# Attention and the first unit's group 0: from separate loops to one list of operations with needs, ranks and durations

## The chip, the cores and the metric

The kernel runs on one core of a Trainium2 chip. The core has a matrix engine (TensorE, PE in the profile, with its weight loads shown apart as PEld), a vector engine (VectorE, DVE), a scalar engine (ScalarE, ACT), a general engine (GpSimd, POOL) and a sync engine (SyncE, SP) that here only issues DMA transfers. Each engine works through its own queue in order and waits at an instruction until the semaphores it needs have come. The metric is the device time of one execution in microseconds: 676.35 us before, the median of 3 runs from 675.85 to 676.41.

## The reference, cut to what matters

Three stages follow one another: windowed attention with a slope per head, a layer of four weighted experts, and a gated layer behind a norm.

```python
# attention: batch 2, heads 8, seq 576, head_dim 64, window 128
scores = scale * np.matmul(q, k.transpose(0, 1, 3, 2))
scores = np.where(mask, scores + bias[None], -1000000000.0)
scores = scores - np.max(scores, axis=-1, keepdims=True)
attn = np.exp(scores)
attn = attn / (np.sum(attn, axis=-1, keepdims=True) + 1e-09)
attn_out = np.matmul(attn, v)
x = attn_out.transpose(0, 2, 1, 3).reshape(1152, 512)
# experts: x (1152, 512), w1 (4, 512, 1024), w2 (4, 1024, 512)
p = domain_probs / (domain_probs.sum(-1, keepdims=True) + 1e-09)
for e in range(4):
    h = np.maximum(x @ w1[e], 0.0)
    out += p[:, e:e + 1] * (h @ w2[e])
# gated layer: rms norm, silu(xn @ w_gate) * (xn @ w_val) @ w_out
```

## The kernel before, in words

**Attention** (lines 297 to 413) goes over 8 pairs of heads, called pair 0 to 7 here: 2 batches times 4 pairs. For each pair, `load_pair` fetches keys and queries (`kt`, `qt`) and, for every second pair, values (`vt`). `scores` takes the 576 rows in 9 row blocks of 64: PE multiplies into the PSUM tile `s` (L337), DVE adds the bias and finds the least value (L346), ACT takes the exponential (L350), DVE makes the reciprocals for 5 and then 4 row blocks (L359, L360), and POOL scales (L362). The rows lie in one of two buffers, `tt` and a part of `y`, in turn. `values` transposes them on PE into `pst` (L383), ACT or DVE copies them out into `pt` and `pe` (L369, L371; which engine is written down as `"dadad"`), and PE multiplies them with the values into `po` (L389) and the end of `pst` (L406). The result is split into two parts, `xh` by ACT (L412) and `xl` by DVE (L413). So PE uses three shapes of its array here: 64*64 for `s`, 128*64 for `po` and the products of L406, and 128*128 for transposes and all that follows.

**Fillers.** Tokens come in two groups of 576, one for each batch. The first half of expert 0 (the first unit) is computed plainly: `hidden` (L226) makes `h` from `x` and `w1`, 12 matmuls of 288 columns into `psa` for each of 8 blocks of group 0, and `mixed` (L419) makes 4 output tiles of 12 matmuls into `psb`, after it has split `h` into two parts, ACT first (L179) and then POOL (L180). The weights are split the same way. Then `sums` (L431) makes 7 operands for the later units out of sums of quarters of `x`: 12 operations of 128x576 on DVE and 4 on ACT, on `scratch`.

**What sets the order.** In this part the code only says in which order things are recorded: pair by pair, scores one pair ahead of values, one of the `sums` behind every second row block, two fillers behind each pair of the second batch, the rest at the end. A scheduler of the language then orders each engine's instructions. Behind the attention a planner (`Plan`, L49) decides, and from the mark at L521 on each of PE, DVE, ACT and POOL is held to the recorded order by added dependencies (L1160 to L1169). The first work behind the attention is group 1 of the first unit: 8 blocks of 12 matmuls into `ps_a` to `ps_d` (by the helper's line, L209), then 5 output tiles (L901), then the units of products (L783).

Of the kernel before, what the change touches and what calls it, by code (L numbers as in the profile page):

```python
# [24 lines left out]
P = 128  # L25
# [120 lines left out]

@with_exitstack
def tile_fused(ctx: ExitStack, tc: tile.TileContext, qS, kS, vS, probs, w1, w2, wgv, wo, g, out):
# [87 lines left out]
    def load_probs():  # L236
        nc.sync.dma_start(out=pr_sb, in_=probs)
        nc.vector.tensor_reduce(out=psm, in_=pr_sb, op=ALU.add, axis=mybir.AxisListType.X)
# [23 lines left out]
    with (  # L262
# [34 lines left out]
        def load_pair(b, p):  # L297
            qt = qk_p.tile([P, S], F32, tag="q", name="qt")
            kt = qk_p.tile([P, S], F32, tag="k", name="kt")
            nc.sync.dma_start(out=kt, in_=kS[b, p])  # L300
            state["dma"] = nc.sync.dma_start(out=qt, in_=qS[b, p])
            if p % 2 == 0:
# [4 lines left out]
                state["vt"] = vt  # L307
            if b == 0:
                for r in range(2):
                    rows = slice(r * D, (r + 1) * D)  # L310
                    for i, eng in enumerate((nc.vector, nc.gpsimd)):
                        eng.tensor_scalar(
                            out=bias[rows, p, i, :], in0=rel[rows], scalar1=-8.0 * 2.0 ** (-8.0 * (2 * p + (r ^ i) + 1) / H),
                            scalar2=1.0, op0=ALU.mult, op1=ALU.mult,
                        )
            return qt, kt, state["vt"]

        def scores(n, p, qt, kt):
            tt = tts[n % 2]
            st = st_p.tile([P, 4, NQ], F32, tag="st", name="st")  # L320
            spans = []
            sps = []

            def pair(t0):

                ts = range(t0, min(t0 + 2, NQ))
                for t in ts:
                    k0 = max(0, t - 2) * D
                    nk = (t + 1) * D - k0
                    sps.append(ps_s.tile([P, 4 * D], F32, tag="s", name="s")[:, :nk])  # L330
                    c0 = WIN - nk + (D if t % 2 else 0)
                    spans.append(tt[:, t, c0 : c0 + nk])
                for t in ts:
                    k0 = max(0, t - 2) * D
                    for r in range(2):
                        rows, o = slice(r * D, (r + 1) * D), (r ^ t & 1) * D
                        nc.tensor.matmul(  # L337
                            sps[t][o : o + D, :], lhsT=qt[rows, t * D : (t + 1) * D], rhs=kt[rows, k0 : (t + 1) * D],
# [3 lines left out]
            for t in range(NQ):  # L342
                if t % 2 == 0:
                    pair(t)
                nk = sps[t].shape[1]
                nc.vector.tensor_tensor_reduce(  # L346
                    out=spans[t], in0=sps[t], in1=bias[:, p, t % 2, WIN - nk :], scale=-0.125, scalar=3.0e38,
                    op0=ALU.add, op1=ALU.min, accum_out=st[:, 0, t : t + 1],
                )
                nc.scalar.activation(  # L350
                    out=spans[t], in_=spans[t], func=AF.Exp, bias=st[:, 0, t : t + 1], scale=-1.0,
                    accum_out=st[:, 1, t : t + 1],
                )
                if t % 2:
                    some(1)
                if t + 1 in (5, 9):
                    g0 = (5, 9)[(5, 9).index(t + 1) - 1] if (5, 9).index(t + 1) else 0
                    gs = slice(g0, t + 1)
                    nc.vector.tensor_scalar(out=st[:, 2, gs], in0=st[:, 1, gs], scalar1=1e-9, scalar2=None, op0=ALU.add)  # L359
                    nc.vector.reciprocal(out=st[:, 3, gs], in_=st[:, 2, gs])  # L360
                    for j in range(g0, t + 1):
                        nc.gpsimd.tensor_scalar(  # L362
                            out=spans[j], in0=spans[j], scalar1=st[:, 3, j : j + 1], scalar2=1.0, op0=ALU.mult, op1=ALU.mult,
                        )
            return tt

        def evac(eng, out, in_):
            if eng == "a":
                nc.scalar.activation(out=out, in_=in_, func=AF.Copy)  # L369
            else:  # L370
                nc.vector.tensor_copy(out, in_)  # L371

        def values(b, p, tt, vt):
            pt = pt_p.tile([P, 4, 4, P], F32, tag="pt", name="pt")
            pe = pt_p.tile([D, P], F32, tag="pe", name="pe")
            po = ps_o.tile([P, 4 * P], F32, tag="po", name="po")
            for kb in range(5):
                n = min(4, NQ - 2 * kb)
                nk = D if kb == 4 else P
                pst = ps_t.tile([P, 4, P], F32, tag="pst", name="pst")  # L380
                for j in range(n):
                    c0 = P if j < 2 else 0
                    nc.tensor.transpose(pst[:nk, j, :], tt[:, 2 * kb + j, c0 : c0 + nk], ident)  # L383
                dst = pe if kb == 4 else pt[:, kb, :n, :]
                evac("dadad"[kb], dst, pst[:nk, 0, :] if kb == 4 else pst[:, :n, :])

                def mm(j, out, rhs, start, stop):
                    v = slice((2 * p % 4 + j) * D, (2 * p % 4 + j + 1) * D)
                    nc.tensor.matmul(  # L389
                        out, lhsT=vt[:nk, kb, v], rhs=rhs, start=start, stop=stop, skip_group_check=True,  # L390
                    )

                if kb < 4:
                    m = 4 if kb < 3 else 2
                    blocks = pt[:, kb, :m, :].rearrange("p (a b) (c d) -> p a (b c) d", b=2, c=2)
                    for j in range(2):
                        r = slice(j * D, (j + 1) * D)
                        mm(j, po[r, kb * P : kb * P + m * D], blocks[:, :, 1:3, :] if j else blocks[:, :, ::3, :], kb == 0, kb == 3)
                else:
                    pp = pst[:, 2, :D]  # L400
                    for kk in (3, 4):
                        for j in range(2):
                            r = slice(j * D, (j + 1) * D)
                            v = slice((2 * p % 4 + j) * D, (2 * p % 4 + j + 1) * D)
                            n = P if kk == 3 else D
                            nc.tensor.matmul(  # L406
                                pp[r, :], lhsT=vt[:n, kk, v], rhs=pt[:, 3, 2, r] if kk == 3 else pe[:, r],
                                start=kk == 3, stop=kk == 4, skip_group_check=True,
                            )
            for ps, w, o in ((po, 4 * P, 0), (pp, D, 4 * P)):  # L410
                c = slice(b * S + o, b * S + o + w)
                nc.scalar.activation(out=xh[:, p, c], in_=ps, func=AF.Copy)  # L412
                nc.vector.tensor_tensor(out=xl[:, p, c], in0=ps, in1=xh[:, p, c].bitcast(F32), op=ALU.subtract)  # L413

        def filler():
            w = blocks["w1_0"]
            v = blocks["w2_0"]

            def mixed(t):  # L419
                a = token_parts(op_p.tile([P, 2, 512], F32R, tag="oa", name="op"), t, "ap")  # L420
                ps = ps_a0.tile([P, DM], F32, tag="a", name="psb")
                gemm_out(ps, a, v)
                nc.vector.tensor_scalar(out=y[:, t, :], in0=ps, scalar1=pn_sb[:, t, :1], scalar2=None, op0=ALU.mult)

            for c in range(4):
                for t0 in (0, 288):
                    yield lambda c=c, t0=t0: hidden(ps_a0, w, c, t0, 288)
            for t in range(4):
                yield lambda t=t: mixed(t)

        def sums():  # L431

            st = [scratch()[:, :S].rearrange("p (a b) -> p a b", a=2) for _ in range(2)]
            (ah, al), (bh, bl), (ch, cl), (dh, dl) = ([x.bitcast(F32) for x in second(n, 0)] for n in (0, 1, 2, 4))

            def tt(op, out, a, b):
                return lambda: nc.vector.tensor_tensor(out=out, in0=a, in1=b, op=op)

            def keep(n, i):
                hi, lo = second(n, 0)  # L440
                yield lambda: nc.scalar.activation(out=hi, in_=st[i], func=AF.Copy)
                yield tt(ALU.subtract, lo, st[i], hi.bitcast(F32))

            yield tt(ALU.subtract, st[0], ch, dh)
            yield tt(ALU.add, st[0], st[0], cl)
            yield tt(ALU.subtract, st[0], st[0], dl)
            yield from keep(6, 0)
            yield tt(ALU.subtract, st[0], dh, ah)
            yield tt(ALU.add, st[0], st[0], dl)
            yield tt(ALU.subtract, st[0], st[0], al)  # L450
# [751 lines left out]
```

## Time and profile before

| what | before |
|---|---|
| time, median of 3 runs | 676.35 us (675.85 to 676.41) |
| the profiled execution's own time | 676.36 us |
| its span, first to last instruction | 674.6 us |
| granted TensorE clock | 1.000 |
| PE busy | 663.5 us (98% of the span) |
| DVE, ACT, POOL busy | 512.8, 312.2, 54.6 us |
| first matmul of group 1 starts (`ps_b`, L209) | 95.81 us |

The first 95.81 us of the span are the part that the change touches; from there on the chain that ended last runs on PE nearly without a break. Busy time of PE is read with care: a matmul counts from its start to its modelled end, matmuls overlap, and a matmul that stands in the array while the next shape waits counts as busy too. So in this part the starts of successive rows say more than the busy share.

### The profile page before, as it was taken

The page shows a single profiled execution, that of the slowest core. Times are in us where ns is not written, and L with a number is a line of the kernel's source. Part 1 is how long each engine was busy: PE and PEld are TensorE (multiplying, and loading weights), DVE is VectorE, ACT ScalarE, POOL GpSimd, SP SyncE. Part 2 cuts the span into 40 slices and gives each one's busy share as a digit, 9 for nine tenths or more (in the row PEclk, how much of TensorE's full clock was granted, in tenths as well). Part 3 has the DMA queues.
Part 4 walks back from the last instruction along what each step waited for, and adds up shares of the span by engine and source line. Part 5 has one row for each costly group of instructions (what it writes and reads, how often), then busy time and mean ns, then how long its engine had stood idle before and what let it go on. Part 6 is the DMA issues. An engine that isn't in the chain of part 4 may idle for free.

```text
span 674.6 us, 11038 instructions
## 1 busy us (share of the span) xinstructions
PE 663.5 (98%) x4168; PEld 585.2 (87%) x4168; DVE 512.8 (76%) x1107; ACT 312.2 (46%) x711; POOL 54.6 (8%) x108
## 2 busy tenths in 40 slices
PE   8999999999999999999999999999999999999997
PEld 4566779998988988989989989879998999889986
DVE  6677568778888888888887888888778368847672
ACT  6876525363543543544634535755246333313320
POOL 7864320000000000000000000000000000000000
PEclk9999999999999999999999999999999999999999
DMA  8550002305551642544525415202011201000012
GB/s 270 173 168 3 0 1 71 127 23 171 188 188 63 197 147 94 190 124 135 184 72 176 152 64 173 79 0 94 33 38 57 79 16 64 1 31 32 33 48 93
DMA packets 23942, 64.95 MB, mean 96 GB/s; under 512 B 2641, under 2 KB 4945, under 8 KB 23889
## 3 DMA queue, kind: packets, MB, share of 16 engines
q1 hardware_dynamic: 23888, 64.25, 29.0%
q8 instruction: 32, 0.52, 0.3%
q14 instruction: 22, 0.17, 0.1%
HBM read 52.45 MB, written 11.80 MB: 95 GB/s over the span
## 4 chain that ended last, share of the span: by engine, by line
PE 96%; DVE 3%; ACT 1%; issue 0%; POOL 0%; POOLq 0%
PE ps_b L901 13%; PE ps_c L783 10%; PE ps_d L783 10%; PE ps_d L901 9%; PE ps_a L901 8%; PE ps_c L901 8%; PE ps_a L783 8%; PE ps_b L783 7%; PE ps_b L209 3%; PE s L337 3%; PE pst L383 3%; PE po L389 2%; PE ps_a L209 2%; PE ps_c L209 2%; PE psa L209 2%; PE ps_d L209 2%
## 5 line engine op out<-in xcount | busy, mean ns | idle before, releaser
L901 PE MATMUL ps_b<-wa,op 128*128 128x512 f32 x372 | 88.3, 390 | 0.0
L538 ACT ACTIVATE op<-h 128x512 fp32r<-128x512 f32 x95 | 57.5, 626 | 58.9 <-PE ps_d L901 27.4
L901 PEld LDWEIGHTS ps_b<-wa,op 128*128 128x128 f32 x372 | 69.2, 188 | 14.1
L538 ACT ACTIVATE wb<-raw 128x512 fp32r<-128x512 f32 (+1 forms) x98 | 49.9, 537 | 46.0 <-DVE raw L531 45.6
L531 DVE TENSOR_TENSOR op<-h,op 128x512 fp32r<-128x512 f32 x95 | 64.0, 685 | 1.9 <-ACT op L538 1.6
L901 PE MATMUL ps_d<-wa,op 128*128 128x512 f32 x276 | 64.9, 390 | 0.0
L901 PEld LDWEIGHTS ps_d<-wa,op 128*128 128x128 f32 x276 | 51.7, 188 | 10.7
L901 PE MATMUL ps_a<-wa,op 128*128 128x512 f32 x252 | 58.9, 389 | 0.0
L531 DVE TENSOR_TENSOR wb<-raw,wb 128x512 fp32r<-128x512 f32 (+1 forms) x98 | 54.6, 575 | 2.3 <-ACT wb L538 1.9
L901 PE MATMUL ps_c<-wa,op 128*128 128x512 f32 x240 | 56.2, 389 | 0.0
L901 PEld LDWEIGHTS ps_a<-wa,op 128*128 128x128 f32 x252 | 47.3, 188 | 9.8
L901 PEld LDWEIGHTS ps_c<-wa,op 128*128 128x128 f32 x240 | 45.0, 188 | 9.4
L531 DVE TENSOR_TENSOR wa<-raw,wa 128x512 fp32r<-128x512 f32 (+1 forms) x50 | 32.0, 653 | 14.3 <-ACT wa L538 14.3
L538 ACT ACTIVATE wa<-raw 128x512 fp32r<-128x512 f32 (+1 forms) x50 | 28.4, 598 | 22.1 <-DMA raw<-in_w 19.9
L783 PE MATMUL ps_c<-xh,wb 128*128 128x288 f32 x160 | 38.6, 297 | 0.0
L783 PE MATMUL ps_d<-xh,wb 128*128 128x288 f32 x160 | 38.6, 296 | 0.0
L783 PE MATMUL ps_a<-xh,wb 128*128 128x288 f32 x160 | 38.3, 294 | 0.0
L783 PE MATMUL ps_b<-xh,wb 128*128 128x288 f32 x160 | 38.2, 294 | 0.0
L844 ACT ACTIVATE h<-r 128x576 f32<-128x576 f32 x28 | 19.2, 686 | 32.4 <-DVE r L534 32.4
L534 DVE TENSOR_TENSOR r<-ps_c,x 128x288 f32<-128x288 f32 x44 | 20.1, 457 | 16.1 <-PE ps_c L783 13.6
L783 PEld LDWEIGHTS ps_b<-xh,wb 128*128 128x128 f32 x160 | 27.8, 188 | 0.4
L534 DVE TENSOR_TENSOR r<-ps_d,x 128x288 f32<-128x288 f32 x44 | 20.1, 457 | 10.5 <-PE ps_d L783 8.7
(258 smaller groups left out, 1550.1 us busy)
## 6 DMA issues: line engine op xcount, KB each, us to landing
raw<-in_w SPq DMA_DIRECT2D x32, 512.0 KB, 3.8
scratch<-in_wgv SPq DMA_DIRECT2D x24, 512.0 KB, 4.3
f<-stage SPq DMA_DIRECT2D x36, 256.0 KB, 2.5
raw<-f SPq DMA_DIRECT2D x18, 512.0 KB, 3.2
scratch<-in_wo SPq DMA_DIRECT2D x12, 512.0 KB, 4.3
kt<-in_kS SPq DMA_DIRECT2D x8, 288.0 KB, 3.5
qt<-in_qS SPq DMA_DIRECT2D x8, 288.0 KB, 3.8
out_y<-acc SPq DMA_DIRECT2D x9, 256.0 KB, 2.0
```

What stands on the lines that cost most here:

```text
L209: nc.tensor.matmul(ps, lhsT=a, rhs=x[:, k, tok], start=(n == 0), stop=(n == 3 * KC - 1))
L337: nc.tensor.matmul(sps[t][o : o + D, :], lhsT=qt[rows, t * D : (t + 1) * D], rhs=kt[rows, k0 : (t + 1) * D], start=True, stop=True,)
L383: nc.tensor.transpose(pst[:nk, j, :], tt[:, 2 * kb + j, c0 : c0 + nk], ident)
L389: nc.tensor.matmul(out, lhsT=vt[:nk, kb, v], rhs=rhs, start=start, stop=stop, skip_group_check=True,)
L531: EN[e].tensor_tensor(out=out, in0=a, in1=b, op=ALU.subtract)
L534: EN[e].tensor_tensor(out=out, in0=a, in1=b, op=ALU.add)
L538: nc.scalar.activation(out=out, in_=a, func=AF.Copy)
L783: nc.tensor.matmul(ps, lhsT=s[:, k, :], rhs=t(k), start=start and m == 0, stop=m == 5, skip_group_check=True,)
L844: return wrote(gr, pl.now("a", tok.stop - tok.start, needs + was_reading[gr], lambda e: nc.scalar.activation(out=h[:, c, tok], in_=src, fu ...
L901: nc.tensor.matmul(ps, lhsT=a(s)[:, k, :], rhs=w[k][0]()[:, i, :], start=(n == 0), stop=(n == 11))
```

## The change

Attention, the fillers and the sums of group 0 are no longer recorded by loops that the scheduler reorders. Each operation is added to a list with the engine (or the engines that could do it), a duration, the operations that it needs and a rank. `Flow.run` plays the list through: at each step it takes, among the operations whose needs are done and that can start within 0.1 us of the earliest on their engine, the one of the lowest rank; an operation of PE that changes the shape of the array is ranked one unit later and charged 0.1 us. The operations are then emitted in the order of their starts, and the mark moves to the front of the attention, so that the added dependencies hold PE, DVE, ACT and POOL to this order. SP is not among those.

Some work is also cut differently. The copies out of `pst` may be done by ACT or DVE, as the list has it. A block of `hidden` comes in two operations of 6 matmuls and needs the `xh` and `xl` of all four pairs of the first batch. An output tile comes in four operations of 3 matmuls, and the second part of its `h` is made by DVE instead of POOL. No matmul is added or removed. The tables of ranks and durations are shown by a line or two.

```diff
+class Flow:
+    LAT = 0.12
+    NEAR = 0.1
+    STAY, SWITCH = 1.0, 0.1
+    MODE = {"s": 1, "o": 2}
+    RANK = dict(q=0.0, b=-1.09, s=-1.2, m=-1.16, n=-1.52, x=0.01, c=-0.6, o=1.53, h=-0.83, w=1.0, f=6.09, r=0.31, g=7.88, u=100.0)
+    def run(self):
+        ends, order, left, mode = {}, [], set(range(len(self.ops))), 0
+        while left:
+            ready = []
+            for i in left:
+                engines, costs, needs, _, (kind, n), _ = self.ops[i]
+                turn = engines == "t" and self.MODE.get(kind, 0) != mode
+                rank = n + self.RANK[kind] + self.STAY * turn
+                if all(n in ends for n in needs):
+                    t = max((ends[n][0] + (0.0 if ends[n][1] == engines else self.LAT) for n in needs), default=0.0)
+                    _, start, e = min((max(self.free[e], t) + costs[e], max(self.free[e], t), e) for e in engines)
+                    ready.append((start, rank, i, e))
...
+            for start, rank, i, e in ready:
+                if start <= first[e] + self.NEAR and (e not in picks or (rank, start, i) < picks[e][:3]):
+                    picks[e] = (rank, start, i)
...
+        for _, _, i, e in sorted(order):
+            self.ops[i][3](e)
...
+        mark = len(tc.nc.cur_bb.bb.instructions)
+        flow = Flow({"t": 4.6, "d": 0.0, "a": 2.0, "p": 5.0, "q": 0.7})
...
+            did["qk", n] = add("q", 1.0, [did.get(("s", n - 2, 8)), did.get(("qk", n - 1))], both, rank, 2.6)
...
+            did["c", n, kb] = c = add("da", cost, [x, *old], out, ("c", n + kb / 10))
...
+                j = add("q", 0.5, [behind, prev["w"]], fetch, rank, 3.2)
...
+                    ends.append(add("p", 1.3, [ja], low, rank))
...
+            for k0 in (0, 2):
+                j = add("t", 0.83, needs + [j, prev["f", 0] if k0 == 0 else None], lambda e, k0=k0: some(e, k0), rank)
...
+            ja = add("a", 0.63, needs + [prev["oa"]], high, rank)
+            jd = add("d", 0.69, [ja], low, rank)
...
+            for k in range(4):
+                j = add("t", 0.7, [jd, j, prev["f", 0] if k == 0 else None] + did["w2"], lambda e, k=k: some(e, k), rank)
...
+            if n == 1:
+                j = add("q", 0.2, [did["qk", 2]], lambda e: load_probs(), ("w", 2), 3.0)
+                did["pn"] = add("d", 0.7, [j], lambda e: norm_probs(), ("w", 2))
+                did["w1"] = weights("w1_0", [w1[0, 0], w1[0, 1]], did["qk", 2], ("w", 2))
+            if n == 3:
+                did["w2"] = weights("w2_0", [w2[0, :, :2, :], w2[0, :, 2:, :]], did["qk", 4], ("w", 4))
+                x0 = [did[w, i] for w in ("ld", "hd") for i in range(4)]
+                hid = [hidden_filler(c, t0, x0 + did["w1"]) for c in range(4) for t0 in (0, HT)]
+                for t in range(4):
+                    out_filler(t, hid)
+                sums(x0, hid[-1])
+        flow.run()
...
-    mark = len(tc.nc.cur_bb.bb.instructions)
```

On PE, at the values of the first pair, the order before is this (`s` are scores, `pst` transposes, `po` products with the values):

```order
L383 MATMUL pst<-ident,tt 128x128 x6
L337 MATMUL s<-kt,qt 64x64 x2
L337 MATMUL s<-kt,qt 64x128 x2
L337 MATMUL s<-kt,qt 64x192
L389 MATMUL po<-pt,vt 64x256 x2
L383 MATMUL pst<-ident,tt 128x128 x4
L337 MATMUL s<-kt,qt 64x192 x3
L389 MATMUL po<-pt,vt 64x256 x2
L383 MATMUL pst<-ident,tt 128x128
L389 MATMUL po<-pt,vt 64x256 x2
L383 MATMUL pst<-ident,tt 128x128 x2
```

and in the change the same place on PE reads (L423 is L337 of before, L485 is L383, L504 is L389):

```order
L485 MATMUL pst<-ident,tt 128x128 x7
L423 MATMUL s<-kt,qt 64x64 x2
L423 MATMUL s<-kt,qt 64x128 x2
L485 MATMUL pst<-ident,tt 64x128
L504 MATMUL po<-pt,vt 64x256 x6
L504 MATMUL po<-pt,vt 64x128 x2
L423 MATMUL s<-kt,qt 64x192 x4
L485 MATMUL pst<-ident,y 128x128 x4
L515 MATMUL pst<-pt,vt 64x64 x2
```

The products of one pair now stand together instead of in three places. Over the whole part, from the first scores to the last product or filler of group 0, the order of before has 111 such runs of one kind on PE, that of the change 85; up to the last product of the fourth pair it is 59 and 40. A run of fillers right behind a run of transposes, or of output fillers behind hidden ones, is the case in 12 of the runs before and in 11 of the change.

On PE at the end of the part, before (`psb` are the output tiles of the first unit, L209 with `ps_b` is the first work of group 1):

```order
L383 MATMUL pst<-ident,y 64x128
L209 MATMUL psa<-xl,wa 128x288
L209 MATMUL psa<-xh,wa 128x288 x2
L209 MATMUL psa<-xl,wa 128x288
L406 MATMUL pst<-pt,vt 64x64 x2
L406 MATMUL pst<-pe,vt 64x64 x2
...
L223 MATMUL psb<-wa,op 128x512 x48
L209 MATMUL ps_b<-xh,wa 128x288
```

and in the change, where L612 is L223 of before:

```order
L612 MATMUL psb<-wa,op 128x512 x9
L485 MATMUL pst<-ident,y 128x128 x4
L612 MATMUL psb<-wa,op 128x512 x3
L485 MATMUL pst<-ident,y 128x128 x7
L612 MATMUL psb<-wa,op 128x512 x3
L485 MATMUL pst<-ident,y 64x128
L612 MATMUL psb<-wa,op 128x512 x15
L504 MATMUL po<-pt,vt 64x256 x6
L504 MATMUL po<-pt,vt 64x128 x2
L515 MATMUL pst<-pt,vt 64x64 x2
L515 MATMUL pst<-pe,vt 64x64 x2
L267 MATMUL ps_b<-xh,wa 128x288
```

The 48 matmuls of the output tiles stood in one row behind the last pair; now they stand among the last two pairs, and the last pair's products are the last of the part. On DVE, eight of the twelve sums stand in one row in the change, between the row blocks 5 and 6 of pair 6, and the last four among the last two pairs; before, the last four stood behind the last pair.

On SP, where the transfers of the second and third pair are issued, before (`raw` are weights as they come from memory, 512 KB each):

```order
L305 DMA vt<-in_vS 128x4x256
L306 DMA vt<-in_vS 64x256
L300 DMA kt<-in_kS 128x576
L301 DMA qt<-in_qS 128x576
L237 DMA pr_sb<-in_probs 128x36
L184 DMA raw<-in_w 128x1024 x2
```

and in the change, where L377 and L378 are the keys and queries and L242 the weights:

```order
L383 DMA vt<-in_vS 128x4x256
L384 DMA vt<-in_vS 64x256
L295 DMA pr_sb<-in_probs 128x36
L242 DMA raw<-in_w 128x1024 x2
L377 DMA kt<-in_kS 128x576
L378 DMA qt<-in_qS 128x576
```

The two weight transfers moved ahead of the keys and queries of the third pair.

## Rows read from the trace of the kernel before

**Rows 1.** Busy time by stretches of 10 us: stretch, PE, PEld, DVE, ACT, POOL.

```profile
70.00:80.00 10.00, 10.00 (x87) 7.62 (x87) 3.24 (x7) 3.80 (x8) 1.92 (x5) 1.00 0.00 0
80.00:90.00 10.00, 7.92 (x41) 6.18 (x41) 9.58 (x9) 4.49 (x9) 6.90 (x4) 1.00 0.01 2
100.00:110.00 10.00, 10.00 (x73) 9.72 (x72) 8.51 (x18) 6.41 (x15) 0.00 (x0) 1.00 0.21 63
```

**Rows 2.** The chain that ended last, around the part's end: start, length, what.

```profile
82.29 1.68 DVE xl L437
...
95.81 1.58 PE ps_b L209 x12
```

**Rows 3.** PE in order of time: start, length, what, wait ahead of it in brackets.

```profile
23.68 0.65 PE L389 MATMUL po<-pt,vt 128*64 128x256 f32 x4 [1.09 <-DVE pt L371]
...
44.59 0.22 PE L406 MATMUL pst<-pe,vt 64*64 64x64 f32 x2
...
83.41 5.29 PE L223 MATMUL psb<-wa,op 128*128 128x512 f32 x22 [0.78 <-POOL op L180]
90.09 5.72 PE L223 MATMUL psb<-wa,op 128*128 128x512 f32 x24 [1.39 <-ACT th L441]
```

**Rows 4.** The same chain, runs of one kind on PE without a wait.

```profile
14.51 0.58 PE po L389 x4
...
28.86 0.59 PE pst L383 x4
...
37.66 1.02 PE pst L383 x8
...
39.86 0.46 PE psa L209 x2
...
50.58 1.45 PE po L389 x12
...
57.67 0.61 PE pst L383 x4
58.28 1.33 PE psa L209 x10
```

**Rows 5.** DVE in order of time.

```profile
21.45 1.59 DVE L359 TENSOR_SCALAR st<-st 128x5 f32<-128x5 f32 x1
...
47.10 0.75 DVE L437 TENSOR_TENSOR scratch<-scratch,xl 128x576 f32<-128x576 f32 x1
47.77 0.35 DVE L346 CUSTOM_DVE_ANT_0 y<-s,bias 128x192 f32<-128x192 f32 x1
...
80.54 0.23 DVE L413 TENSOR_TENSOR xl<-pst,xh 128x64 fp32r<-128x64 f32 x1 [0.23 <-ACT xh L412]
```

**Rows 6.** POOL in order of time, merged by line.

```profile
30.59 1.86 POOL L362 TENSOR_SCALAR y<-y,st 128x64 f32<-128x64 f32 x5 [1.29 <-DVE st L360]
...
47.14 3.02 POOL L362 TENSOR_SCALAR y<-y,st 128x64 f32<-128x64 f32 x5 [5.12 <-PE pst L383]
...
81.76 6.90 POOL L180 TENSOR_TENSOR op<-h,op 128x512 fp32r<-128x512 f32 x4 [9.84 <-ACT op L179]
```

**Rows 7.** SP's DMA issues in order of time.

```profile
1.65 0.43 SPq L305 DMA_DIRECT2D vt<-in_vS  x1
...
9.22 0.43 SPq L301 DMA_DIRECT2D qt<-in_qS  x1
...
10.17 0.90 SPq L184 DMA_DIRECT2D raw<-in_w  x2
```

**Rows 8.** The page's DMA list: KB each, median us from issue to landing.

```profile
qt<-in_qS SPq DMA_DIRECT2D x8, 288.0 KB, 3.8
vt<-in_vS SPq DMA_DIRECT2D x4, 512.0 KB, 5.0
```

**Rows 9.** Stretches as in rows 1; the last two columns are DMA share, GB/s.

```profile
5.00:10.00 5.00, 3.93 (x43) 2.10 (x45) 3.70 (x24) 3.69 (x17) 3.57 (x11) 1.00 0.96 301
```

**Rows 10.** The same chain, first scores of the third and the last pair.

```profile
13.92 0.58 PE s L337 x7
...
63.52 0.59 PE s L337 x8
```

More of the change, by code (lines that the diff above doesn't have):

```diff
@@ L337, in pair, with before @@
                         nc.tensor.matmul(
-                            sps[t][o : o + D, :], lhsT=qt[rows, t * D : (t + 1) * D], rhs=kt[rows, k0 : (t + 1) * D],
+                            sps[n, t][o : o + D, :], lhsT=qts[n][rows, t * D : (t + 1) * D], rhs=kts[n][rows, k0:k1],
                             start=True, stop=True,
                         )
[L342 to L345, printed above, removed]
+            def before(t):
+                q = NQ * n + t - 3
+                return did.get(("m", q // NQ, q % NQ)) if q >= 0 else None
@@ L346, in scores, with softmax, least @@
+            j = add("t", 0.38 if len(ts) == 2 else 0.33, [did["qk", n], prev["s"], *map(before, ts)], emit, ("s", n + t0 / 20))
+            prev["s"] = j
+            for t in ts:
+                did["s", n, t] = j
+        def softmax(n, t):
+            b, p = order[n]
+            def least(e):
+                if t == 0:
+                    sts[n] = st_p.tile([P, 4, NQ], F32, tag="st", name="st")
+                nk = sps[n, t].shape[1]
                 nc.vector.tensor_tensor_reduce(
-                    out=spans[t], in0=sps[t], in1=bias[:, p, t % 2, WIN - nk :], scale=-0.125, scalar=3.0e38,
@@ L354, in scores @@
[L354 to L363, printed above, removed]
-                        )
@@ L365, in scores @@
[L365 to L400, printed above, removed]
@@ new lines, in exp @@
+                    out=span_of(n, t), in_=span_of(n, t), func=AF.Exp, bias=sts[n][:, 0, t : t + 1], scale=-1.0,
+                    accum_out=sts[n][:, 1, t : t + 1],
+                )
+            slopes = [did["b", p, r, t % 2] for r in range(2)]
+            did["m", n, t] = add("d", 0.42, [did["s", n, t], did.get(("x", n - 2, min(t // 2, 4))), did.get(("n", n - 4, NQ - 1)), did.get(("m", n, 0))] + slopes, least, ("m", n + t / 20))
+            did["e", n, t] = add("a", 0.46, [did["m", n, t]], exp, ("m", n + t / 20))
@@ L494, in tile_fused @@
-        while queue:
-            values(*queue.pop(0))
-        for i, f in enumerate(todo):
-            f()
-            if i >= 1:
-                some(3)
-        some(99)
+            did["x", n, kb] = x = add("t", 0.109 * m + 0.03, [prev["x"], *free] + [did["n", n, 2 * kb + j] for j in range(m)], transposes, ("x", n + kb / 10))
+            prev["x"] = x
+            old = [did.get(("o", n - 2, 3)), did.get(("o", n - 2, 4))] if kb == 0 else [did["c", n, 0]]
+            cost = {4: {"d": 0.68, "a": 0.6}, 3: {"d": 0.55, "a": 0.5}, 1: {"d": 0.29, "a": 0.25}}[m]
@@ new lines, in tile_fused @@
+        prev = dict.fromkeys(["s", "x", "o", "w", "wa", "oa", ("f", 0), ("f", 1), ("f", 2)])
+        load(0)
+        for n in range(len(order)):
+            if n + 1 < len(order):
+                load(n + 1)
+            for t0 in range(0, NQ, 2):
+                pair(n, t0)
+                for t in range(t0, min(t0 + 2, NQ)):
+                    softmax(n, t)
+                if t0 == 4:
+                    norm(n, 0, 5)
+                if t0 == 8:
+                    norm(n, 5, 9)
+            for kb in range(5):
+                values(n, kb)
+                if kb == 3:
+                    pass
+            halves(n)
+            if n == 1:
[9 more added lines that the diff above has]
+                sums(x0, hid[-1])
```

308 lines of the change are left out of this document (207 added, 101 removed).

## The prediction

> **What bounds the kernel now.** I read the chain of waits first: from 95.81 us on, where group 1 begins, it hardly leaves PE. So the question is when PE comes to that matmul. The stretches come next [rows 1]: from 70 to 80 us PE is full while DVE and ACT work 3.24 and 3.80 us of 10; from 80 to 90 it is the other way round, DVE 9.58, PE 7.92. The part does first what PE has to do and then what DVE has to do. Its end is the second of these: at 82.29 the chain is in the last sums on DVE [rows 2], and it comes back to PE only at 90.09, for the second half of the output tiles [rows 3]. PE stood still twice in that stretch, 0.78 us for the second parts of `h` from POOL and 1.39 us because ACT's queue had a sum in it that waited for DVE [rows 3].
>
> Ahead of that PE is busy by the page, but not because it streams all the time. Rows of different length give what a run costs beyond its matmuls [rows 4]: 8 transposes take 1.02 us and 4 take 0.59, so one more costs 0.1075 and 4 carry 0.59 - 4 x 0.1075 = 0.16 us that is not theirs; for products with the values, 12 at 1.45 and 4 at 0.58 give 0.109 each and 0.145 besides. Fillers behind transposes carry none (10 in 1.33, 0.133 each), behind another kind they do (2 in 0.46, 0.20 besides). A run of one kind costs PE about 0.16 us.
>
> **The change part by part.** Terms are against the profiled execution's own time, 676.36 us (a span of 674.6 and 1.76 around it); the median of the runs, 676.35, is the same. No matmul comes or goes, so on PE only runs, stops and waits count.
>
> *Fewer runs on PE.* 111 runs become 85; less those that carry nothing (12 and 11, fillers behind transposes or fillers), 99 become 74. 25 x 0.16 = 4.0 us less. 19 of them lie ahead of the end of the fourth pair, 6 behind it. Bounds: 6 x 0.16 = 1.0, if PE waits there anyway in the early pairs and the charge hides in the wait; 25 x 0.18 = 4.5 above, by the dearest row: 4 transposes at 0.61 us right behind fillers [rows 4], 0.61 - 0.43.
>
> That row is one of no change of shape: transposes and fillers are both 128*128. The Trainium skill (TensorEngine Tiling (Array Packing), Key Properties) says that changing the tiling mode, and not merely the tile, drains TensorE; by it only changes of shape would cost, and these go from 92 to 63, 29 x 0.16 = 4.6 us. By that rule, the trace agrees for scores and products but not for this transition, so the sum goes by the rows.
>
> *The end of the part.* The 48 matmuls of the output tiles, about 11 us, move from behind the last pair to among the last two, where DVE and ACT had room [rows 1]; the second parts of `h` go from POOL to DVE. The two stops, 0.78 + 1.39 = 2.2 us, go with it [rows 3]: the new row has 15 output matmuls (3.6 us at 5.72/24 = 0.24 each) between the last transposes and the last products, longer than the copies that these products wait for. Bounds 0 and 2.2; I take 2.2. What is late next is the last pair itself: from its first scores at 63.52 to its last `xl` at about 80.8 it took 17.2 us [rows 5, 10]. In the new order its first scores have behind them 48 output matmuls (11.4), the last pair's own matmuls and most of pair 6's, some 20 us of PE work, so its chain has room. DVE gets 4 more subtractions, 4 x 0.6 = 2.4 us, in a stretch where it was idle 6.8 of 10; at no cost. Three sums of group 1 that DVE did before 95.81 come after it, 3 x 0.67 = 2.0 us; DVE is not full in that stretch either [rows 1], and their first use lies in the third product of the next unit; no cost, 2.0 at most.
>
> *Weights no longer in the way on ACT.* The 1.09 us for which PE waited near 23 us [rows 3] goes back to DVE, held for 1.59 us at a reciprocal's first step [rows 5] that waited for exponentials, ahead of which ACT split weights two at a time. The new order spaces these. Bounds 0 and 1.1; I take 0.5.
>
> *Weights ahead of keys on SP.* This goes against the change. Before, the queries of the third pair were issued at 9.22 and the weights behind them at 10.17 [rows 7]; with 3.8 us to landing [rows 8] they were there at about 13.0, and the first scores ran at 13.9 [rows 10]. Now two weight transfers stand ahead. They wait for nothing that PE does and can issue when the first transfers have landed: the values issued at 1.65 were there 5.0 us later [rows 7, 8]. The keys still wait for pair 0's scores, until about 9.2. The DMA engines were 0.96 full then at 301 GB/s [rows 9], so 2 x 512 KB take 1.05 MB / 301 GB/s = 3.5 us, and the keys behind them land at up to 13.0 + 3.5 = 16.5. PE comes to their scores about 14.6, since the new row has 15 transposes ahead of them instead of 8 (7 x 0.1075 = 0.75 after 13.9). So PE waits 0 to 1.9 us, with the last transpose and the products of pair 0 queued behind it; I charge 1.2, two thirds of the most, as DVE, ACT and POOL still have work of the first two pairs then.
>
> *Early fillers.* Before, 10 hidden matmuls (1.3 us) ran ahead of the end of the fourth pair, in gaps; now none can, since they need all four pairs. As long as PE is the bound this is only moved; if the early pairs wait on other engines it costs 1.3. I take 0. The copies that change between DVE and ACT cost nothing, both being about half free.
>
> Sum: -4.0 - 2.2 - 0.5 + 1.2 = -5.5, so 676.36 - 5.5 = 670.9 us.
>
> **The rivals.** *The gain is lost early (no change).* If the first four pairs are paced by the chain through DVE, ACT and POOL and not by PE, 19 of the 25 runs are worth nothing, the late keys cost 1.2 and the missing fillers 1.3: -1.0 - 2.2 + 1.2 + 1.3 = -0.7, so 675.7. For it: PE's waits on DVE at 23.68 and the late keys. Against: POOL loses the splits of half the weights in this stretch, and the new row lets a pair overlap two others.
>
> *The sums go slow (slower).* Eight sums in one row on DVE stand ahead of pair 6's last three row blocks. At the pace of 47.10 to 47.77 they take 8 x 0.67 = 5.4 us [rows 5], under 60 filler matmuls on PE (60 x 0.133 + 0.6 = 8.6 us). But next to POOL's subtractions, from 81.76 on [rows 6], a sum took 1.68 us [rows 2]. Then the eight take 13.4, PE waits 13.4 - 8.6 = 4.8 at its scores, and of the four later ones two stand ahead of the last pair's copies, 2 x 1.0 more: 670.9 + 6.8 = 677.7. The gain is used up from about 1.5 us a sum on. What has to happen is that POOL's own subtractions, three of the weights just ahead of pair 6's scalings, slide beside the sums. Against it: beside POOL's scalings a sum stayed at 0.75 us [rows 5], and it was POOL that went from 1.86 to 3.02 for five [rows 6]. The Trainium skill (SBUF — State Buffer, Who interferes with whom) has it that a DVE instruction with two SBUF inputs contends with any GpSimd instruction that reads SBUF. By that rule the eight sums and the scalings would hold each other up; the trace shows the cost on POOL's side there.
>
> *The order does not hold.* The row is fixed by dependencies on four engines and can be read in the built program; only SP is outside, which is the term above.
>
> **How the numbers follow.** Forecast, with its own range of 667.0 to 674.0: 0.75. Gain lost early, 675.7: 0.15. Slow sums, 677.7: 0.08. The rest, 0.02, is an end below 666.5. The low end takes the best bounds, -4.5 - 2.2 - 1.1 and no late keys, 668.6, and as much as the two stops at the end again for smaller waits that no row names: 666.4, rounded to 666.5. The high end goes most of the way to the case of no change: 675.2. That case lies on both sides of the line below. A measurement of this kernel tells 0.2%, 1.35 us, from no change, so faster means below 675.0: 0.78 (the forecast, and a little of the lost gain); same 0.13; slower 0.09.
>
> **What would show it.** The first matmul of group 1 near 90.3 us instead of 95.81 [rows 2], and everything behind it earlier by the same. No wait of PE ahead of output matmuls. A wait of PE of 1 to 2 us for DMA at the third pair's first scores. Sums at 0.75 us each in pair 6. The fourth pair's last product near 42.5 us instead of 44.6 [rows 3] if the early runs are worth what I say (19 x 0.16 = 3.0, less 1.2, and 0.5 from ACT); near 46 if they are not. I am wrong if PE waits as long within the last two pairs as it saved, or if the work behind 95.81 does not move along.

## Result: 667.93 us, 8.4 us less than before

| what | before | the change |
|---|---|---|
| median of 4 runs each | 676.38 us (675.85 to 676.41) | 667.93 us (667.77 to 668.04) |
| ratio, with its 95% interval | 1 | 0.9876 (0.9861 to 0.9891) |
| span of the profiled execution | 674.6 us | 666.2 us |
| first matmul of group 1 in PE's timeline | 95.65 us | 87.12 us |

The forecast was 670.9 us, its range 666.5 to 675.2: faster, as said, but by 8.4 us instead of 5.5. Behind the first matmul of group 1 everything moved along: it starts 8.5 us earlier, and the span is 8.4 shorter.

PE's timeline of the change (start, length, what, the wait ahead of it in brackets) shows all the waits that it lists behind 5 us, and the last products of the first and the fourth pair:

```profile
6.97 4.43 PE L423 MATMUL s<-kt,qt 64*64 64x192 f32 x40 [0.96 <-DVE st L444]
...
18.99 0.23 PE L515 MATMUL pst<-pe,vt 64*64 64x64 f32 x2
...
26.79 0.65 PE L504 MATMUL po<-pt,vt 128*64 128x256 f32 x4 [0.62 <-DVE xl L539]
...
39.22 0.23 PE L515 MATMUL pst<-pe,vt 64*64 64x64 f32 x2
...
85.61 0.33 PE L515 MATMUL pst<-pe,vt 64*64 64x64 f32 x4
87.12 0.40 PE L267 MATMUL ps_b<-xh,wa 128*128 128x288 f32 x1 [1.18 <-DVE xl L539]
```

The fourth pair ends at 39.22 instead of 44.59 [rows 3]: 5.4 us ahead, of which 1.3 are the ten filler matmuls that come later now (10 x 0.133). The two stops of [rows 3] at the end of the part are gone, as is the 1.09 at 23.68. Two new ones stand in their place, both behind an `xl` on DVE: 0.62 at 26.79, and 1.18 right ahead of group 1, where nothing is left on PE to do. All of PE's waits from 5 us to group 1 were 4.5 us before (seven) and are 2.8 now (three).

The stretches that answer to [rows 1], with the same columns: DVE's 9.58 us of 10 next to the end has become 8.50 one stretch earlier.

```profile
70.00:80.00 10.00, 10.00 (x77) 7.61 (x75) 8.50 (x25) 5.10 (x17) 4.75 (x9) 1.00 0.00 0
80.00:87.00 7.00, 5.94 (x42) 4.32 (x40) 3.39 (x8) 1.26 (x3) 0.00 (x0) 1.00 0.01 2
```

The sums in pair 6, on DVE, and what POOL did beside them. (The trace has fourteen sums on DVE, not twelve: three ahead of this row, seven in it, four behind.)

```profile
54.91 0.81 DVE L632 TENSOR_TENSOR tl<-scratch,th 128x576 fp32r<-128x576 f32 x1 [0.46 <-ACT th L638]
55.76 0.86 DVE L632 TENSOR_TENSOR scratch<-xh 128x576 f32<-128x576 f32 x1
...
58.45 0.76 DVE L632 TENSOR_TENSOR scratch<-xh,scratch 128x576 f32<-128x576 f32 x1
```

```profile
50.20 3.83 POOL L562 TENSOR_TENSOR wa<-raw,wa 128x512 fp32r<-128x512 f32 x3
54.46 3.35 POOL L468 TENSOR_SCALAR tt<-tt,st 128x64 f32<-128x64 f32 x5 [0.42 <-DVE pe L369]
```

POOL's weights were done at 54.03, before this row began. Beside the scalings a sum took 0.81 to 0.88 us, alone 0.76; five scalings took 3.35 us instead of 1.86 [rows 6]. The slow row of sums didn't come.

### The profile page after: what moved, and what is told of

Read it like the earlier page. It is cut to its first block, busy times and chain, and to the rows that moved or that the text cites. A ratio compares the mean times of both kernels' runs of the same rounds, so it can differ in the third digit from the quotient of the medians.

```text
span 666.2 us, 11039 instructions
## 1 busy us (share of the span) xinstructions
PE 656.9 (99%) x4168; PEld 585.1 (88%) x4168; DVE 511.1 (77%) x1104; ACT 314.6 (47%) x718; POOL 48.9 (7%) x104
## 4 chain that ended last, share of the span: by engine, by line
PE 96%; DVE 2%; ACT 0%; issue 0%; POOL 0%; POOLq 0%; DVEq 0%
PE ps_b L1085 13%; PE ps_c L967 11%; PE ps_d L967 11%; PE ps_d L1085 9%; PE ps_a L1085 9%; PE ps_c L1085 8%; PE ps_a L967 8%; PE ps_b L967 7%; PE ps_b L267 3%; PE pst L485 2%; PE s L423 2%; PE ps_a L267 2%; PE ps_c L267 2%; PE po L504 2%; PE psa L583 2%; PE psb L612 2%
## 5 line engine op out<-in xcount | busy, mean ns | idle before, releaser
L722 ACT ACTIVATE wa<-raw 128x512 fp32r<-128x512 f32 (+1 forms) x50 | 28.4, 597 | 21.7 <-DMA raw<-in_w 19.5
```

Of the source, the lines that this page charges most:

```text
L722: nc.scalar.activation(out=out, in_=a, func=AF.Copy)
```

## Experiments

Two theories. *Shapes*: PE pays whenever the shape of its array changes, and the rest of the gain is stops at the part's end. *Waits*: what counts is whether the order has work for PE while DVE, ACT and POOL finish what it needs next; fewer changes are a side effect. The expectations of the first ten kernels count changes with every transpose as 128*128 (92 to 63). The traces show a transpose of 64 rows as 128*64; so counted they are 99 and 78, and the text below uses these.

### What a change of shape costs

The patterns, of matmuls that are in no result:

```diff
+ N = 8
...
+ for text in ("x" * N, "s" * N, "o" * N, "f" * N, "xs" * N, "xo" * N, "so" * N, "xf" * N, "sf" * N, "of" * N):
+     for c in text:
+         runs[c]()
```

> The change, with matmuls put in front that are in no result: runs of one kind (x: 4 transposes of 128x128, s: 4 matmuls 64*64 of 192 columns, o: 2 matmuls 128*64 of 256, f: 6 matmuls 128*128 of 288), each kind first alone and then in turn with another, 8 runs a pattern. No other engine takes part. If only a change of shape costs, the mixed patterns with s or o take about 0.15 us a run more than the mean of the two kinds alone, and x in turn with f takes nothing more. If a change of kind costs, x with f takes 0.16 a run more as well.

One run (743.78 us, with the patterns in it). The start of each pattern, and the end of the last, in PE's timeline; the last row is the first four transposes by themselves, with the shortest, median and longest in ns (273 for nearly all behind them):

```profile
4.76 4.06 PE L366 MATMUL ps<-ident,y 128*128 128x128 f32 x32
8.75 2.83 PE L371 MATMUL pa<-y 64*64 64x192 f32 x64
11.51 3.67 PE L375 MATMUL pb<-y 128*64 128x256 f32 x32
15.11 6.59 PE L379 MATMUL pf<-xh 128*128 128x288 f32 x48
21.54 0.60 PE L366 MATMUL ps<-ident,y 128*128 128x128 f32 x4
...
30.07 0.66 PE L366 MATMUL ps<-ident,y 128*128 128x128 f32 x4
...
39.42 0.56 PE L371 MATMUL pa<-y 64*64 64x192 f32 x8
...
47.97 0.66 PE L366 MATMUL ps<-ident,y 128*128 128x128 f32 x4
...
57.94 0.56 PE L371 MATMUL pa<-y 64*64 64x192 f32 x8
...
69.71 0.65 PE L375 MATMUL pb<-y 128*64 128x256 f32 x4
...
82.29 2.79 PE L451 MATMUL s<-kt,qt 64*64 64x64 f32 x36
```

```profile
L366 PE MATMUL ps<-ident,y x4: 361/421/421, 4.8 to 5.4; 128*128 128x128 f32 x4
```

A pattern by 8 is not yet a run alone. The first four transposes took 0.84 us, every later four 0.44, and the last run of a pattern holds the change into the next one. So I take the runs between, from start to start: x 0.437, s 0.325, o 0.432, f 0.790 us. What a pair of a mixed pattern takes beyond its two runs, taken in the same way (six pairs, the first and the last left out), is two changes:

| pattern | a pair | its runs alone | a change |
|---|---|---|---|
| x s | 1.073 | 0.762 | 0.16 |
| x o | 1.169 | 0.869 | 0.15 |
| s o | 1.068 | 0.757 | 0.16 |
| x f | 1.228 | 1.227 | 0.00 |
| s f | 1.470 | 1.115 | 0.18 |
| o f | 1.573 | 1.222 | 0.18 |

From transposes to fillers, both 128*128, nothing is paid. Every change of shape costs 0.15 to 0.18 us, 0.163 in the mean of the five. The Trainium skill (TensorEngine Tiling (Array Packing), Key Properties) says that a change of the tiling mode drains TensorE; the patterns agree, against my reading of a row: the mode counts, not the kind of run. 21 x 0.163 = 3.4 us of the 8.4.

### The end of the part

The last pair's stop, covered:

```diff
-                j = add("t", 0.7, [jd, j, prev["f", 0] if k == 0 else None] + did["w2"], lambda e, k=k: some(e, k), rank)
+                j = add("t", 0.7, [jd, j, prev["f", 0] if k == 0 else None] + did["w2"], lambda e, k=k: some(e, k), ("g", 5) if t == 3 and k >= 2 else rank)
```

> The change, with one edit: of the last output tile's four operations the last two (6 matmuls of 128x512, 1.4 us) stand behind the last pair's products instead of ahead of them. In the trace of the change PE stands still for 1.18 us ahead of the first matmul of group 1, which waits for the last xl on DVE. If that stop is a wait for the last pair's copies, the 6 matmuls cover it: -1.2 us against the change (667.9), so 666.7, and the first matmul of group 1 near 85.9 instead of 87.12. If PE is held back there by something that comes along (the two more changes of shape cost 0.3, or the wait is for the output tile's own bank), the time stays at 667.9 to 668.2.

Measured 666.51 us (666.5 to 666.75), ratio 0.9860 (0.9843 to 0.9876): 1.4 less than the change, and the fastest kernel of this study. In PE's timeline the six matmuls stand between the last products and group 1, and the stop is gone:

```profile
84.03 0.33 PE L515 MATMUL pst<-pe,vt 64*64 64x64 f32 x4
84.29 1.66 PE L612 MATMUL psb<-wa,op 128*128 128x512 f32 x6
85.78 0.29 PE L267 MATMUL ps_b<-xh,wa 128*128 128x288 f32 x1
```

So it was a wait for the last pair's copies. (The group's first matmul waits for the last `xl` either for its data or for the PSUM that it is read from; this doesn't tell which.)

The second parts of `h` on DVE, in the kernel before:

```diff
-a = token_parts(op_p.tile([P, 2, 512], F32R, tag="oa", name="op"), t, "ap")
+a = token_parts(op_p.tile([P, 2, 512], F32R, tag="oa", name="op"), t, "ad")
```

> The kernel before, with one edit: the second parts of h for the output tiles are made by DVE, as the change has it, with the loops and the scheduler as they were. The two stops at the end of the part, 0.78 and 1.39 us, stood at POOL's second part and at a sum on DVE beside it. If these stops go back to POOL and DVE in each other's way, they go: -0.8 to -2.2, so 674.2 to 675.6 against 676.4. If DVE is simply full there (9.58 us of 10 busy), four more subtractions on it (4 x 0.6 = 2.4 us) make the second stop longer: 676.4 to 678.0.

673.76 us (673.51 to 673.78), ratio 0.9964 (0.9950 to 0.9977): 2.3 less from one letter, with the order as it was. On DVE, in this kernel, a sum beside a subtraction, and on PE the output tiles, which now run without a stop:

```profile
82.33 0.75 DVE L437 TENSOR_TENSOR xl<-scratch,xh 128x576 fp32r<-128x576 f32 x1
83.00 0.68 DVE L180 TENSOR_TENSOR op<-h,op 128x512 fp32r<-128x512 f32 x1
```

```profile
82.01 11.17 PE L223 MATMUL psb<-wa,op 128*128 128x512 f32 x48
93.03 0.29 PE L209 MATMUL ps_b<-xh,wa 128*128 128x288 f32 x1
```

The same sum took 1.68 us in [rows 2], beside POOL's 6.90 us for four subtractions [rows 6]; DVE does them in 0.68 each, and its sums are back at 0.75. The second stop, behind a sum, was those two engines in each other's way. In the first, behind POOL's own subtraction, its pace alone has a share (1.27 to 1.29 us, next run); how much isn't told apart. The rule of the Trainium skill (SBUF — State Buffer, Who interferes with whom) that I set against a row of scalings holds here; how much each side pays depends on what POOL does: beside the scalings in pair 6 a sum took 0.81 to 0.88.

The same parts back on POOL, in the change:

```diff
-                nc.vector.tensor_tensor(out=tile[0][:, 1], in0=h[:, :, t * P : (t + 1) * P], in1=tile[0][:, 0].bitcast(F32), op=ALU.subtract)
+                nc.gpsimd.tensor_tensor(out=tile[0][:, 1], in0=h[:, :, t * P : (t + 1) * P], in1=tile[0][:, 0].bitcast(F32), op=ALU.subtract)
```

> The change, with one edit: the second parts of h for the four output tiles are made by POOL again, as before (L600), in the same planned order on every other engine. If the part's end term was a matter of where the output tiles stand on PE, POOL has time for them: within 0.3 us of 667.9. If POOL's subtractions beside the sums slow both (6.90 us for four on POOL and 1.68 a sum on DVE before), PE waits at output matmuls or at the last pairs' scores: 0.8 to 5 us more, 668.7 to 673.

668.31 us (668.25 to 668.62), +0.4. In the new order each subtraction stands alone on POOL (1.27 to 1.29 us each), and PE has one new wait, of 0.29, for a scaling behind them. So either edit removes the stops: another engine, or another place.

The output tiles' matmuls behind the last pair again, by rank:

```diff
-box, rank = [], ("g", 0)
+box, rank = [], ("g", 90)
```

> The change, planned with one other number: the output tiles' matmuls have the last rank, so that most of them (24 of 48 in one row) stand behind the last pair's products, as before. 84 runs on PE instead of 85, 69 changes of shape instead of 63. If only the changes count: 6 x 0.16 = +1.0, less the stop of 1.18 that is covered, -0.2: 667.7. If runs of any kind count: -0.2 - 1.2 = -1.4, 666.5. If the place of these matmuls carries the 2.2 us that the prediction gave to the part's end (DVE and ACT late behind the last pair): +1 to +2.2, 669 to 670.

668.04 us (667.87 to 668.17), +0.1. 24 matmuls stand behind the last pair, the stop ahead of group 1 is gone, and a transpose waits 0.49 us for POOL in the last pair instead. By the shapes in the trace it has 78 changes, as many as the change. With the subtractions off POOL, the place of these matmuls is worth nothing in the sum: the 1.18 that it covers at the end is lost again ahead of it, 0.49 of it in that wait.

### The early pairs

Keys first on SP:

```diff
-                nc.sync.dma_start(out=qts[n], in_=qS[b, p])
+                keyed[n] = nc.sync.dma_start(out=qts[n], in_=qS[b, p])
...
-                    raws[name, i] = load_raw(src)
+                    if name == "w1_0":
+                        with tc.issue_after(keyed[2].ins):
+                            raws[name, i] = load_raw(src)
+                    else:
+                        raws[name, i] = load_raw(src)
```

> The change, with one edit: on SP the keys and queries of the third pair are issued ahead of the two weight transfers, as before. By the prediction's term (keys that land 0 to 1.9 us late, 1.2 charged) the time falls by 1.2 us, to 666.7, and the third pair's scores come that much earlier than 15.13. By the trace of the change (the scores run at 15.13 right behind transposes, no wait for DMA) nothing is gained: 667.9 within 0.3, or up to 0.6 more if the weights' splits come late and push ACT's copies.

667.85 us (667.74 to 667.98): no difference. In the change SP issued the weights at 5.69 and the queries at 10.31, and its DMA list has 4.4 us to landing for these (the median of all queries): 14.7, and PE came to their scores at 15.13.

The bias work of later pairs behind the first least values, alone and with the covered end:

```diff
-        for _, _, i, e in sorted(order):
+        seq = sorted(order)
+        late = [x for x in seq if x[3] == "d" and self.ops[x[2]][4][0] == "b" and self.ops[x[2]][4][1] > 0]
+        seq = [x for x in seq if x not in late]
+        at = next(j for j, x in enumerate(seq) if x[3] == "d" and self.ops[x[2]][4] == ("m", 2 / 20)) + 1
+        for _, _, i, e in seq[:at] + late + seq[at:]:
```

> The change, with one edit: the seven additions on DVE that prepare the bias of pairs 1 to 3, which stand ahead of the first least-value operation of pair 0, stand behind the third of them. In the trace of the change the first least value begins at 6.69 us, before at 5.42. If the first pairs are paced by this start, the time falls by up to 1.2 us, 667.9 to 666.7, and the fourth pair's last product comes about 1.2 earlier than 39.22. If PE's own work and its changes of shape set the pace from the first transposes on, the start is caught up: within 0.3 us of 667.9.

> Both of the last two edits. The stops lie 50 us apart and on different engines, so the gains should add: 665.5 if both hold (-1.2 -1.2), 666.7 if only the end does. The stop ahead of group 1 must not come back, since what is moved at the start moves the end rigidly.

668.75 us (668.56 to 670.64) alone and 667.43 (667.33 to 668.25) with the end covered: 0.8 and 0.9 slower, where -1.2 or 0 was expected. The first least value did begin at 5.42 instead of 6.69, but the bias work, 2.12 us, now stands ahead of the fourth. Of the kernel with this edit alone, stretches with the columns of [rows 1]; the figure behind POOL's is the granted clock:

```profile
8.00:10.00 2.00, 1.09 (x12) 0.58 (x12) 1.45 (x9) 1.11 (x5) 0.08 (x1) 1.00 1.11 351
10.00:12.00 2.00, 1.41 (x18) 1.10 (x16) 1.57 (x12) 1.73 (x9) 1.49 (x5) 0.59 1.02 397
12.00:16.00 4.00, 4.00 (x31) 2.38 (x28) 1.74 (x12) 2.90 (x12) 2.00 (x5) 0.50 0.38 149
16.00:18.00 2.00, 2.00 (x23) 1.29 (x17) 1.06 (x5) 1.29 (x7) 0.00 (x0) 0.71 0.24 35
```

PE had waited 1.69 and 0.59 us, and the clock fell to 0.50 (1.2 GHz) until about 17 us. In the kernel with the keys first, whose order on PE is the change's, the waits there were 0.96 and 0.73, and it stayed at 1.00. The first pair ended at 21.7 in this execution (its time 670.6, the longest of its runs), in the change at 19.0. How much of the loss is the clock's and how much the wait's own stays open.

### The planner's rule and the fixed order

No preference for the shape that PE is in:

```diff
-    STAY, SWITCH = 1.0, 0.1
+    STAY, SWITCH = 0.0, 0.0
```

> The change, planned without the two numbers that hold a shape (an operation of another shape isn't ranked later and isn't charged). 90 runs on PE instead of 85, 82 changes of shape instead of 63. If each change of shape costs 0.16 us: 19 x 0.16 = +3.0, 670.9. If each run of a kind costs 0.16: 5 x 0.16 = +0.8, 668.7. If the gain is a matter of the fixed order and of waits on other engines, neither: 667.9 within 0.5.

677.01 us (674.99 to 678.21), ratio 1.0014 (1.0005 to 1.0023): the whole gain is lost, 9.1 us, with 86 changes instead of 78, 8 x 0.163 = 1.3. The plan is another one: between the ends of the fourth and the fifth pair 12 hidden matmuls run instead of 24, and PE waits for the other engines there, in its timeline:

```profile
35.22 0.65 PE L504 MATMUL po<-pt,vt 128*64 128x256 f32 x4 [1.08 <-DVE xl L539]
...
46.92 0.33 PE L485 MATMUL pst<-ident,tt 128*128 128x128 f32 x1 [2.35 <-POOL tt L468]
47.19 1.12 PE L504 MATMUL po<-pt,vt 128*64 128x256 f32 x4
```

On POOL, ahead of that scaling, stands a part of the weights that waited 3.42 us for ACT. Behind the wait the granted clock was 0.72 from 46 to 52 us, and the products in the last row took 1.12 us, those in the first 0.65. The fourth pair ends at 40.1, only 0.9 later than in the change; the other 7.9 us are lost behind it.

The list, but not held to it:

```diff
-        mark = len(tc.nc.cur_bb.bb.instructions)
         flow = Flow({"t": 4.6, "d": 0.0, "a": 2.0, "p": 5.0, "q": 0.7})
...
+    mark = len(tc.nc.cur_bb.bb.instructions)
```

> The change, with one edit: the mark stays at its old place behind the attention, so that the list gives the order in which the work is recorded, and the scheduler may reorder it. The program has 95 runs on PE instead of 85 and 73 changes of shape instead of 63. By 0.16 us a change or a run: +1.6, 669.5. If the fixing itself matters more (waits that the free order brings, as the stops at the end of the part before): 671 to 675. If neither, 667.9.

678.0 us (677.5 to 680.4), ratio 1.0031 (1.0019 to 1.0043): 10 us more than the change. On DVE:

```profile
6.35 0.08 DVE L443 DVE_READ_ACCUMULATOR2_ANT st<- 128x1 f32 x1
10.94 0.19 DVE L298 TENSOR_REDUCE psm<-pr_sb 128x9 f32<-128x36 f32 x1 [4.51 <-DMA pr_sb<-in_probs]
```

The scheduler put the expert probabilities ahead of all but three of pair 0's least values, and they waited for their DMA. PE stood 4.79 us, and its clock fell:

```profile
8.00:10.00 2.00, 0.00 (x0) 0.00 (x0) 0.00 (x0) 0.00 (x0) 0.31 (x1) 1.00 1.10 386
10.00:20.00 10.00, 7.79 (x56) 4.20 (x56) 4.70 (x33) 6.24 (x25) 3.49 (x9) 0.50 0.36 130
20.00:30.00 10.00, 9.81 (x100) 5.85 (x96) 6.68 (x35) 8.62 (x32) 5.66 (x15) 0.99 0.26 66
```

The first pair ends at 25.5 instead of 19.0: 6.5 of the 10 us come from one place, the wait and the 10 us at 0.50 behind it. I tried to take it away by fetching the probabilities two pairs later:

```diff
             if n == 1:
-                j = add("q", 0.2, [did["qk", 2]], lambda e: load_probs(), ("w", 2), 3.0)
-                did["pn"] = add("d", 0.7, [j], lambda e: norm_probs(), ("w", 2))
...
             if n == 3:
+                j = add("q", 0.2, [did["qk", 4]], lambda e: load_probs(), ("w", 4), 3.0)
+                did["pn"] = add("d", 0.7, [j], lambda e: norm_probs(), ("w", 4))
```

> The change with the mark at its old place (678.0 us, its list free to be reordered), and one more edit: the expert probabilities are fetched and normed two pairs later, beside the weights of the fourth pair. In the trace of the free order DVE stood 4.51 us at the first of these operations, waiting for its DMA, ahead of 15 of pair 0's 18 least values; PE waited 4.79 there. If that one misplaced wait is most of the loss: -4.5 to -5, 673.0 to 673.5, and 5 us remain for the small waits of the free order. If the free order loses in many places and this one would be caught up: 676 to 678. If it is all: 668.

681.31 us (677.32 to 681.94). The edit missed: the free scheduler put them there again (13.14 us, a wait of 4.79 for the DMA). It tells only that the list's order did not survive unheld; what the free order costs without this wait stays open.

The loops' order, held:

```diff
+        mark = len(tc.nc.cur_bb.bb.instructions)
+
         def load_pair(b, p):
...
-    mark = len(tc.nc.cur_bb.bb.instructions)
```

> The kernel before, with one edit: the mark stands at the front of the attention, so that PE, DVE, ACT and POOL are held to the order in which the loops of before record the work, and the scheduler can't reorder it. By array shapes as the traces show them (a transpose of 64 rows is 128*64) PE has 78 changes of shape then, as many as the change, where before has 99. If changes of shape alone make the gain: 21 x 0.14 = 3.0 less, 673. If holding an order is what helps, whatever it is: 668 to 672. If what matters is that the order covers the waits for DVE, ACT, POOL, this one doesn't (four transposes, then at once the products that need their copies; a copy takes 0.7 us, 4 such places in each of 8 pairs): 32 x 0.5 to 0.7 = 16 to 22 less the 3: 689 to 695.

770.36 us (767.03 to 771.4), ratio 1.1387: far worse than any case, with as few changes of shape as the change (78). PE's waits up to group 1 (in total, times, longest) and two stretches:

```profile
PE po L391 <- DVE pt L373: 20.4, 16, 2.7
PE s L339 <- DVE st L348: 14.0, 14, 4.6
PE po L391 <- ACT pt L371: 10.5, 16, 0.7
```

```profile
20.00:60.00 40.00, 25.95 (x161) 12.89 (x161) 16.17 (x61) 14.18 (x48) 12.66 (x24) 0.61 0.21 71
60.00:100.00 40.00, 28.09 (x161) 13.66 (x159) 13.52 (x57) 15.18 (x50) 12.49 (x22) 0.54 0.22 71
```

The 32 places that I priced at 0.5 to 0.7 cost 30.9 us, and the scores another 14. The rest of the 94 lies in stretches in which the clock was between 0.54 and 0.80, up to 180 us; how much of it is the clock's isn't told apart. This speaks against the shapes alone, and for the waits: few changes and a fixed order help only if that order covers them.

## Why the prediction was right in sign and short by 3 us

- *Fewer runs on PE, -4.0.* The step that failed is the count: 25 runs, because the row at 57.67 seemed to charge a change from fillers to transposes [rows 4]. Its 0.61 us was a piece of the chain, which runs to the modelled end of the last transpose, 58.28, though the fillers behind it began at 58.04; from start to start the same four transposes take 0.41. Right are 21 changes of shape at 0.163: -3.4. The price, 0.16, was right.
- *The end, -2.2.* The two stops went, and the term held; either of its two edits is enough (POOL's subtractions moved, in the old order: -2.3; the matmuls moved, with the subtractions on POOL: no stop either). "What is late next is the last pair itself ... its chain has room" failed: its last `xl` is late by 1.18 us ahead of group 1. Net -1.0; with six matmuls moved, -1.4 more is to be had.
- *Weights on ACT, -0.5.* 1.09 gone, 0.62 new: -0.5. That the number fits is luck, since the new wait is another one, behind an `xl`.
- *Keys late, +1.2.* Nothing came of it. The weights were issued at 5.69, not at 6.65 as I had them, and the DMA moved 387 GB/s from 8 to 10 us, not the 301 of [rows 9]. The queries landed at 14.7, 0.4 us ahead of their scores, and putting them first gained nothing.
- *Early fillers, 0.* Right in the sum. But the mark for the fourth pair, 42.5, left out that their 1.3 us leave that stretch (and by its own terms, 44.6 - 3.0 + 1.2 - 0.5, it was 42.3). With that and without the keys it would have been 39.8; 39.2 was measured.
- *The rest.* This is the step that cost most: small waits of PE, which the sum put at nothing and which stood only as a margin at the low end of the range. -3.4 for changes and -1.7 for listed waits (4.5 to 2.8) leave 3.4 of the 8.5 us, in starts that come 0.1 to 0.3 us after what the matmuls before need, behind rows whose modelled ends hide the wait. One such place before, on PE and on DVE:

```profile
10.55 2.57 PE L337 MATMUL s<-kt,qt 64*64 64x192 f32 x28
```

```profile
11.50 0.35 DVE L346 CUSTOM_DVE_ANT_0 y<-s,bias 128x192 f32<-128x192 f32 x1
...
11.86 0.33 DVE L346 CUSTOM_DVE_ANT_0 y<-s,bias 128x192 f32<-128x192 f32 x1
...
12.15 0.36 DVE L346 CUSTOM_DVE_ANT_0 y<-s,bias 128x192 f32<-128x192 f32 x1
```

Alone on PE these 28 scores take 28/8 x 0.325 = 1.14 us. Here they took 2.50 from start to start, with no wait listed: from 11.56 on (then 11.91, 12.26, 12.58) a row block's scores began 0.04 us after DVE was done with an earlier one. With the prices of the patterns for every run and every change, PE took 11.0 us more than alone from the first scores to group 1 before, and 5.7 in the change, listed waits included. All of that lies in runs with a matmul that began within 0.08 us of another engine's release (56 runs before, 26 in the change); the others took no more than alone, and even 2.1 and 1.3 us less in total, so the prices are a little high for them. So the rest is waiting for other engines too.

- *Rivals.* The gain was not lost early: 5.4 us of it lie ahead of the fourth pair's end, though hardly any ahead of the first's (19.12 before, 18.99 now). The sums were not slow. "That the order does not hold" did not come about, but it was the right worry: not held, the list gained nothing, and 6.5 of the 10 us were one misplaced wait.

## What to carry to other kernels

Count on PE the changes of array shape, as the trace names the array, not the runs of a kind, and measure their price alone, in the middle of a long pattern: here 0.15 to 0.18 us. Read PE's waits from start to start, since modelled ends hide the small ones. An order by hand pays when it has PE work for each wait on the other engines, and here only when it was held; the last stage needs such work too, so keep a few independent matmuls for the end.

## What the runs showed of the hardware that I had not expected

A wait of PE can be paid twice, since the clock may fall behind it. Behind 4.79 us of it the granted clock was 0.50 for some 10 us, behind 1.69 and 0.59 for some 7, and four transposes took 1.11 us instead of 0.66. In one execution of the kernel with the parts back on POOL the first wait was 1.91 instead of 0.96, and the clock was 0.50 from 8 to 10 us there too. Behind 0.96 and 0.73, in the kernel with the keys first, it stayed at 1.00.

The figure for the clock has to be checked against the matmuls. The stretches of the change say 1.00 from the start, but its scores of 192 columns took longer at first than the same ones in the kernel with the keys first (first row the change, second row keys first; shortest, median and longest in ns):

```profile
L423 PE MATMUL s<-kt,qt x24: 524/524/579, 7.0 to 9.4; 64*64 64x192 f32 x24
```

```profile
L423 PE MATMUL s<-kt,qt x24: 322/348/374, 7.0 to 8.8; 64*64 64x192 f32 x24
```

They are as long as in the stretch at 0.50 of the kernel with both edits (524 too), and down to 322 from 10.8 us on. So in that execution PE ran at the slower level up to about 10.6 us; its first pair ended at 18.99, with the keys first at 18.76.
